# Each load of q, k and v issued as two transfers of four heads

## The chip, the cores and the metric

The kernel runs on one core of a Trainium2 chip. The metric is the device time of one execution in microseconds (us), the median of several runs. Profiles are of one execution each. Engines are named as in the profile: PE (TensorE, matmuls; PEld its weight loads), DVE (VectorE), ACT (ScalarE), POOL (GpSimd) and SP (SyncE, here only an issuer of DMAs). DMAs issued by POOL and by SP are moved by the same 16 transfer engines.

## The reference

Block attention with a Sinkhorn-sorted choice of blocks, and then a token-mixing MLP on its output. Batch B = 4, heads H = 8, sequence S = 768, head size D = 64, 8 blocks of 96 positions.

```python
P = sort_net                                   # [B, H, 8, 8]
for _ in range(5):
    P = exp(P - max(P, -1)); P = P / sum(P, -1); P = P / sum(P, -2)
k_sorted = einsum('bhij,bhjcd->bhicd', P, k blocks)
v_sorted = einsum('bhij,bhjcd->bhicd', P, v blocks)
attn = softmax(scale * q_block @ k_sorted_block^T)
x = (attn @ v_sorted_block) as [B, S, H*D]
wq, wk = x @ w_q, x @ w_k
mixed = (scale * wq @ wk^T) @ x
out = relu(mixed) @ w_out                      # [4, 768, 512], float32
```

## The kernel before

All of q, k and v is read from HBM once, a batch element at a time: twelve loads (`Qn`, `Kn`, `Vn` for each of four batch elements), each of eight heads by 768 positions by 64, float32 in HBM and bfloat16 on the chip. A load puts its 128 partitions by 8 heads by 384 elements into one tile. Each of the three tensors has three buffers (`NIN = 3`), so the load of batch element 3 takes the buffers of element 0 again.

The Sinkhorn steps run on a 32 x 64 tile `Pm` on DVE and ACT (`u_a`, `u_c`, lines 164 to 184) and end in the transposes `PbT`. Meanwhile POOL fills constants (`u_i`): the identity `idb`, zero columns, ones, and at the end `Lx` (lines 194 and 195), which spreads P over partitions. PE meanwhile runs 40 filler matmuls on a zero tile `fil` (`u_Z`). Then `spread` (`u_B`) multiplies `PbT` by `Lx` into PSUM; DVE makes from it the mixing tiles `M` of batch element 0 (`u_n`, `spread_m`, line 233), and ACT copies the rest to `PTR`, from which POOL makes the `M` tiles of the later elements, two heads at a time.

After that PE does, for two heads at a time (a unit `n` of 0 to 3 covers heads 2n and 2n+1): `u_Q` transposes Qn, `u_K` and `u_V` multiply Kn and Vn by `M` (sorting the blocks), `u_F` transposes V back, `u_S` makes scores, ACT exponentiates them (`u_e`), `u_P` multiplies by V, DVE normalises (`u_x`). For batch elements 0 and 1 `u_V` works per pair of heads; for 2 and 3 it reads all eight heads of a third of the rows. Then follow the MLP's units (`u_T`, `u_J`, `u_W`, `u_G`, `u_H`, `u_O`) and the output.

The order is written out by hand in `ORDER` (lines 18 to 51). Each item is unit, batch element, part, and engine or PSUM bank: `l0.1@P` is the load of K for batch element 0 on POOL (0 = q, 1 = k, 2 = v). Every engine works through its own items in that order. The loads stand on POOL's queue in the order K0, V0, Q0, Q1, K1, V1, K2, Q2, then the two weights `wqk` (`m0.0`, `m0.1`), V2, Q3, K3, V3 and the weight `wo` (`m0.2`). Between them stand POOL's constants and its `M` tiles: M of `n1.3` before K1; `n2.0` after it; `n1.0` after V1; `n1.2` after K2; `n1.1`, `n2.1` and `n2.2` after Q2; `n2.3` after wqk; `n3.0` after K3; `n3.3`, `n3.1` and `n3.2` after wo.

The framework adds the waits: a reader of a tile waits for its writer, a writer for the readers before it. For the completions of POOL's DMAs it has eight semaphores, which the DMAs take in turn; an issue whose semaphore has been used before waits on POOL until the DMA that used it has landed.

The end of the kernel (from line 465) checks the row sums and, only if one is out of range, computes all again in another way; in the profiled executions that branch is not taken.

Of the kernel before, what the change touches and what calls it, by code (L numbers as in the profile page):

```python
# [56 lines left out]
def kernel(  # L57
# [11 lines left out]
    nc = tc.nc  # L69
    B, H, S, D = q.shape  # L70
# [3 lines left out]
    P = 128  # L74
# [32 lines left out]
    NIN = 3  # L107
# [129 lines left out]

    def u_l(b, n, e):
        t, src = (Qn, Kn, Vn)[n], (q, k, v)[n]
        nc.gpsimd.dma_start(out=t[b % NIN].rearrange("p h r d -> p h (r d)"),  # L240
                            in_=src[b].rearrange("h (p r) d -> p h (r d)", p=P))

    def u_m(b, n, e):
        if n < 2:
# [206 lines left out]
    for item in ORDER.split():  # L451
        kind, b, n, arg = UNIT.match(item).groups()
        b, half = int(b), halves.get(n[-1], ())
# [22 lines left out]
    with tc.If(redo > 0, preferred_fallthrough_block=False):  # L476
# [12 lines left out]
        for b in range(B):  # L489
            for n in range(3):  # L490
                nc.gpsimd.dma_start(out=(Qn, Kn, Vn)[n][0].rearrange("p h r d -> p h (r d)"),
                                    in_=(q, k, v)[n][b].rearrange("h (p r) d -> p h (r d)", p=P))
            if b == 0:
                spread(1, 0, H)
                src = PS[:, 1, 0:NB * H].rearrange("p (i h) -> p h i", h=H)
            else:
                src = PTR.rearrange("p i h -> p h i")[:, (b - 1) * H:b * H, :]
# [84 lines left out]
```

## Time and profile before

| what | value |
|---|---|
| time, median of 3 runs | 108.27 us (107.89 to 108.35) |
| time of the profiled execution | 108.6 us |
| its span, first to last instruction | 106.8 us |
| mean granted TensorE clock | 0.981 |
| DMA packets and bytes | 18501, 18.57 MB, mean 174 GB/s |
| queue of POOL's DMAs (q0) | 14064 packets, 10.09 MB, 62.8% of 16 engines' span |
| instruction queue (q8) | 14 packets, 0.23 MB |
| loads of K, V, Q: issue to landing, median | 12.8, 14.7 and 15.1 us |

A page begins with the busy share of each engine; a second part cuts the span into 40 slices and gives the busy tenths of each engine and of the DMA engines. The chain that ended last is followed back from the last instruction, at each step to what released it; its shares say which engine sets the end. A line of a timeline has the start, the time taken, engine, source line, operation, tiles (out <- in), how many were merged, and in brackets the idle time of the engine before it and what ended that. A line of the waits has who waited, for whom, the sum in us, how often, and the longest. "issue" there means that the profile shows nothing that the engine waited for. Many lines of PE carry line 149, a helper through which all matmuls go; there the tiles tell them apart.

### The profile page before, as it was taken

The page shows a single profiled execution, that of the slowest core. Times are in us where ns is not written, and L with a number is a line of the kernel's source. Part 1 is how long each engine was busy: PE and PEld are TensorE (multiplying, and loading weights), DVE is VectorE, ACT ScalarE, POOL GpSimd, SP SyncE. Part 2 cuts the span into 40 slices and gives each one's busy share as a digit, 9 for nine tenths or more (in the row PEclk, how much of TensorE's full clock was granted, in tenths as well). Part 3 has the DMA queues.
Part 4 walks back from the last instruction along what each step waited for, and adds up shares of the span by engine and source line. Part 5 has one row for each costly group of instructions (what it writes and reads, how often), then busy time and mean ns, then how long its engine had stood idle before and what let it go on. Part 6 is the DMA issues. An engine that isn't in the chain of part 4 may idle for free.

```text
span 106.8 us, 3637 instructions
## 1 busy us (share of the span) xinstructions
PE 94.2 (88%) x1556; PEld 65.7 (61%) x1556; DVE 74.1 (69%) x144; ACT 69.9 (65%) x101; POOL 31.3 (29%) x51
## 2 busy tenths in 40 slices
PE   5999989597698979889999999999999999999600
PEld 2334489486686966779868867597666565454300
DVE  2687689198797785788989977999767765455200
ACT  4101079769687879898879798688933448784400
POOL 5999089999229400000000000000077000000000
PEclk9999999999999999999999999999999999999975
DMA  0899999999999999999975373100059145496950
GB/s 3 91 201 205 203 203 210 200 203 205 205 204 204 188 202 211 198 203 208 205 161 159 94 211 96 44 6 0 6 196 388 45 196 203 160 408 236 381 196 18
DMA packets 18501, 18.57 MB, mean 174 GB/s; under 512 B 1840, under 2 KB 16560, under 8 KB 18480
## 3 DMA queue, kind: packets, MB, share of 16 engines
q0 software_dynamic: 14064, 10.09, 62.8%
q1 hardware_dynamic: 4416, 8.19, 22.0%
q8 instruction: 14, 0.23, 0.9%
q14 instruction: 7, 0.06, 0.1%
HBM read 20.19 MB, written 6.29 MB: 248 GB/s over the span
## 4 chain that ended last, share of the span: by engine, by line
PE 80%; ACT 6%; issue 4%; DVE 3%; DVEq 0%; ACTq 0%
PE ps L149 80%; ACT E L339 3%; DVE X L364 1%; ACT Vs L153 1%; DVE KT L155 1%; ACT XT L153 1%; ACT QT L153 1%; ACT ot L153 1%; DVE M L233 0%; DVE wk L155 0%; DVE fil L170 0%; DVE RS L362 0%; DVE Pm L169 0%; DVEq L155 0%; ACTq L153 0%
## 5 line engine op out<-in xcount | busy, mean ns | idle before, releaser
L339 ACT ACTIVATE E<-ps 96x960 bf16<-96x960 f32 (+1 forms) x28 | 24.6, 905 | 2.9 <-PE ps L149 2.6
L149 PE MATMUL ps<-wo,mixT 128*128 128x512 bf16 (+1 forms) x100 | 22.9, 371 | 0.0
L364 DVE TENSOR_TENSOR X<-ps,RS 96x896 bf16<-96x896 f32 (+1 forms) x20 | 20.1, 1007 | 0.7
L149 PEld LDWEIGHTS <-mixT 128*128 128x128 bf16 x100 | 8.9, 98 | 8.6 <-issue 0.2
L153 ACT COPY ot<-ps 128x512 f32<-128x512 f32 (+1 forms) x16 | 8.8, 560 | 8.1 <-PE ps L149 4.7
L468 POOL TENSOR_SCALAR ok<-RS 96x280 bf16<-96x280 f32 x1 | 0.9, 924 | 41.9 <-DVE RS L362 41.9
L149 PE MATMUL ps<-fil 128*128 128x512 bf16 x40 | 11.7, 466 | 1.2 <-DVE fil L170 1.2
L149 PE MATMUL ps<-VT,E 96*128 96x65 bf16 x256 | 11.2, 194 | 1.4 <-DVE X L364 0.8
L149 PEld LDWEIGHTS <-E 96*128 96x128 bf16 x256 | 9.8, 97 | 3.6 <-issue 1.5
L149 PE MATMUL ps<-QT,KT 64*128 64x96 bf16 x256 | 9.9, 204 | 1.6 <-issue 1.3
L233 POOL TENSOR_TENSOR M<-PTR,m_p 128x256 bf16<-128x256 bf16 x12 | 8.8, 750 | 7.4 <-PE ps L149 4.1
L155 DVE COPY ot<-ps 128x512 f32<-128x512 f32 x9 | 6.1, 691 | 6.1 <-PE ps L149 3.2
L149 PEld LDWEIGHTS <-fil 128*128 128x128 bf16 x40 | 4.5, 116 | 7.9 <-issue 3.8
L153 ACT CAST KT<-ps 128x768 bf16<-128x768 f32 x10 | 7.7, 805 | 2.0 <-PE ps L149 1.9
L149 PEld LDWEIGHTS <-KT 64*128 64x128 bf16 x256 | 6.8, 94 | 2.9 <-issue 1.6
L149 PE MATMUL ps<-idb,X 96*128 96x96 bf16 x128 | 7.5, 206 | 0.6 <-issue 0.6
L149 PE MATMUL ps<-M,Kn 128*64 128x128 bf16 x192 | 7.5, 221 | 0.3 <-issue 0.3
L155 DVE COPY QT<-ps 128x768 bf16<-128x768 bf16 x13 | 6.7, 551 | 1.4 <-PE ps L149 1.1
L425 ACT ACTIVATE mixT<-ps 128x1024 bf16<-128x1024 f32 x7 | 7.0, 1026 | 0.9 <-PE ps L149 0.6
L149 PEld LDWEIGHTS <-X 96*128 96x128 bf16 x128 | 6.2, 98 | 1.9 <-issue 0.9
L155 DVE COPY VT<-ps 96x1024 bf16<-96x1024 bf16 x7 | 4.8, 687 | 3.5 <-PE ps L149 2.7
L149 PE MATMUL ps<-idb,Qn 128*64 128x128 bf16 x192 | 7.0, 220 | 0.1
(78 smaller groups left out, 154.0 us busy)
## 6 DMA issues: line engine op xcount, KB each, us to landing
out_dram<-ot SPq DMA_DIRECT2D x9, 512.0 KB, 2.8
Kn<-in_k_dram POOLq DMA_DIRECT2D x4, 768.0 KB, 12.8
Vn<-in_v_dram POOLq DMA_DIRECT2D x4, 768.0 KB, 14.7
Qn<-in_q_dram POOLq DMA_DIRECT2D x4, 768.0 KB, 15.1
VT<-Vs SPq DMA_DIRECT2D x12, 130.0 KB, 2.5
out_dram<-ot SPq DMA_DIRECT2D x6, 256.0 KB, 2.7
wo<-in_moe_w_out_dram POOLq DMA_DIRECT2D x1, 512.0 KB, 22.7
qD<-qkT SPq DMA_DIRECT2D x6, 48.0 KB, 2.6
```

Source lines behind the costliest of these rows:

```text
L149: nc.tensor.matmul(o, w, x, is_transpose=t, start=start, stop=stop, skip_group_check=True)
L153: nc.scalar.copy(o, i)
L155: nc.vector.tensor_copy(o, i)
L233: ENG[e].tensor_tensor(out=M[b % 2][:, h0:h1], in0=src[:, h0:h1].unsqueeze(2).to_broadcast([P, 2, SP, NB]), in1=m_p.unsqueeze(1).unsqueeze ...
L339: nc.scalar.activation(E[b % 2][:, n, 0:2 * w * BLK].rearrange("p (t a c) -> p a t c", a=2, c=BLK), PS[0:BLK, bank:bank + 2, 0:w * BLK].re ...
L364: nc.vector.tensor_mul(xo.rearrange("p (a t d) -> p a t d", a=2, d=D), ps[:, :, :, 0:D], rs.unsqueeze(3).to_broadcast([BLK, 2, w, D]))
L425: nc.scalar.activation(o, i, ACT.Relu)
L468: nc.gpsimd.tensor_scalar(out=okf, in0=rsf, scalar1=1e-30, scalar2=None, op0=ALU.is_ge)
```

## The change

`u_l` issues each load as two transfers, heads 0 to 3 and heads 4 to 7, one right behind the other on POOL, in place of one. `ORDER`, tiles, buffers and all else stay.

```diff
     def u_l(b, n, e):
         t, src = (Qn, Kn, Vn)[n], (q, k, v)[n]
-        nc.gpsimd.dma_start(out=t[b % NIN].rearrange("p h r d -> p h (r d)"),
-                            in_=src[b].rearrange("h (p r) d -> p h (r d)", p=P))
+        for h in range(0, H, H // 2):
+            nc.gpsimd.dma_start(out=t[b % NIN][:, h:h + H // 2].rearrange("p h r d -> p h (r d)"),
+                                in_=src[b][h:h + H // 2].rearrange("h (p r) d -> p h (r d)", p=P))
```

The twelve loads become 24 transfers. The branch that computes all again has its own loads, which stay whole.

## The prediction

> **What bounds the kernel now.** I read the page first: the busy shares, the DMA row of the 40 slices, and the chain that ended last.
>
> ```profile
> PE 94.2 (88%) x1556; PEld 65.7 (61%) x1556; DVE 74.1 (69%) x144; ACT 69.9 (65%) x101; POOL 31.3 (29%) x51
> ...
> DMA  0899999999999999999975373100059145496950
> ...
> PE 80%; ACT 6%; issue 4%; DVE 3%; DVEq 0%; ACTq 0%
> ```
>
> TensorE (PE) is 80% of the chain that sets the end. The transfer engines are as good as full from slice 3 to slice 20, some 5 to 53 us, but no DMA stands in the chain: the loads are dense, and yet nobody on the chain waits for one. Whether that is so has to be checked load by load, so I read PE's timeline where each load is used first.
>
> ```profile
> 12.86 0.37 PE L149 MATMUL ps<-PbT,Lx 32*128 32x16 bf16 x8
> 13.62 1.20 PE L149 MATMUL ps<-M,Vn 128*64 128x128 bf16 x36 [0.40 <-DVE M L233]
> 14.63 0.53 PE L149 MATMUL ps<-M,Kn 128*64 128x128 bf16 x12
> ...
> 16.77 0.86 PE L149 MATMUL ps<-idb,Qn 128*64 128x128 bf16 x24
> ...
> 18.57 0.68 PE L149 MATMUL ps<-QT,KT 64*128 64x96 bf16 x23
> 20.54 0.20 PE L149 MATMUL ps<-QT,KT 64*128 64x96 bf16 x1 [1.29 <-issue]
> ...
> 22.02 1.20 PE L149 MATMUL ps<-idb,Qn 128*64 128x128 bf16 x36
> ...
> 26.78 1.20 PE L149 MATMUL ps<-M,Kn 128*64 128x128 bf16 x36
> ```
>
> Issue time plus time to landing, load by load from the DMA view, gives K0 8.7, V0 12.6, Q0 16.4, Q1 21.1, K1 24.9, V1 28.7, K2 32.7, Q2 36.6, V2 41.4, Q3 45.3, K3 49.1 and V3 53.0 us. First uses on PE: V0 13.62 (it waited for M of VectorE, not for V), K0 14.63, Q0 16.77, Q1 22.02, K1 26.78, V1 30.73, K2 39.28, Q2 40.23, V2 45.27, Q3 50.99 and V3 56.11. Every load is there before its use, Q0 by only 0.3 us. PE's waits that follow no engine are these:
>
> ```profile
> PE ps L149 <- issue: 3.2, 5, 1.3
> PE ps L149 <- DVE fil L170: 1.2, 1, 1.2
> PE ps L149 <- DVE X L364: 0.8, 1, 0.8
> ```
>
> The five "issue" gaps (1.29, 0.58, 0.40, 0.56 and 0.32 us) lie 128 weight loads apart, at 20.5, 26.5, 32.5, 39.0 and 45.0 us. Each follows the move of a 16 KB packet on the instruction queue (one starts at 18.22, 24.24, 30.21, 36.62 and 42.65), so PE there waits for its own next block of instructions, whose fetch shares the engines with the loads. None comes after the loads end. Last, GpSimd (POOL), which issues all loads:
>
> ```profile
> 1.29 1.13 POOL L240 DMA_DIRECT2D Kn<-in_k_dram  x1 [0.84 <-POOLq L566]
> ...
> 3.03 0.92 POOL L240 DMA_DIRECT2D Vn<-in_v_dram  x1
> 3.94 0.88 POOL L240 DMA_DIRECT2D Qn<-in_q_dram  x1
> ...
> 8.18 0.88 POOL L240 DMA_DIRECT2D Qn<-in_q_dram  x1
> 9.04 0.54 POOL L194 MEMSET Lx<- 32x512 bf16 x1
> 9.66 0.83 POOL L195 TENSOR_SCALAR_AFFINE_SELECT Lx<-Lx 32x512 bf16<-32x512 bf16 x1
> 13.66 0.75 POOL L233 TENSOR_TENSOR M<-PTR,m_p 128x256 bf16<-128x256 bf16 x1 [3.17 <-ACT PTR L153]
> ...
> 22.34 0.81 POOL L246 DMA_DIRECT2D wqk<-in_moe_w_q_dram  x1
> 23.15 0.75 POOL L246 DMA_DIRECT2D wqk<-in_moe_w_k_dram  x1
> ```
>
> POOL works without a pause from 1.29 to 10.49, where Lx is done. Lx is what PE needs at 12.86. That is the one place where more issuing work on POOL lies near the path.
>
> **What the change gains.** The first four heads of each load land about half a load earlier. Loads land 3.86 us apart, so that is 1.9 us. By the list above nobody waits for any load, so this gain is worth 0. What hides it is PE's own work; if that cover were gone, Q0 would be the first to matter, by its 0.3 us. The bytes, the number of data packets and their order stay as they are. POOL issues its first transfer some 0.15 us sooner (half of the first load), and that too goes to landings that nobody waits for.
>
> **What it adds on POOL.** Twelve more issues. No row shows a half load of four heads, so its price is bounded by the nearest rows. Whole loads (eight rows of 128) cost 0.88 to 0.95 us, the first one 1.13; the three transfers with four rows of 128, wqk twice and wo, cost 0.81, 0.75 and 0.77, mean 0.78. Lower end: 0.46, a whole load divided, with no net cost. Upper end: 0.94, a half as dear as a whole. The shape is that of the wqk and wo rows, so I stay with them; whole loads before 10 us cost about 4% less than later ones, so a half there is 0.75, and the first one 0.98.
>
> Up to Lx that is K0 1.73 for 1.13, V0 1.50 for 0.92, Q0 and Q1 1.50 for 0.88 each: +0.60 +0.58 +0.62 +0.62 = +2.42 us. Lx is then done at 10.49 + 2.42 = 12.91, and PE sees it 0.05 later (M of VectorE ends at 13.57, PE starts at 13.62): 12.96 in place of 12.85, where PE came free of its fillers. **Cost on the path: +0.11 us.** Eight halves at 0.81 make it 0.48 more, +0.59; at 0.73 or less it is nothing. Behind the first Lx matmul stand the M tiles and then all of PE's stream, so a delay here goes to the end one to one.
>
> Lx moves along VectorE's chain, too. The tensor_tensor of L180 at 9.81 took 0.72 us, 0.21 elsewhere; it ended 0.04 after POOL's affine_select of Lx. With Lx's select from about 12.1 on, it meets no two-operand operation of the Sinkhorn chain (the last would end near 11.8), and PbT is ready at 12.1 instead of 12.63. That is worth 0, since the fillers hold PE to 12.85. If the select came early enough to catch L182, PbT would still be there by about 12.8.
>
> The Trainium skill ("SBUF — State Buffer", Who interferes with whom) has a rule for this row: a VectorE instruction with two SBUF inputs and a GpSimd instruction that reads SBUF exclude each other for a whole instruction; by it 0.51 us comes off that chain, and the sum stays the same.
>
> **The new waits.** The program's order shows eight semaphores, taken in turn, for POOL's transfers. Before, the ninth transfer is wqk; now it is the first half of K1, and each issue waits for the landing of the eighth transfer before it. Walking POOL's queue with 0.78 per half and the landings above: K1, V1, K2 and Q2 find theirs landed (Q2's second half asks for Q1, 21.1, at about 22.4). Then the second half of V2 waits until 28.7, Q3 until 30.7 and 32.7, K3 until 34.6 and 36.6, V3 and wo no longer. Queued behind them are M tiles: n1.1 ends near 24.0 (19.4 before) and K1 of those heads is used near 27.5; n2.3 near 27.6, used from 45.3; the last of batch 3 near 42.7 (36.0 before), used from 55.2 (K3). The nearest slack is 3.5 us, so 0. Seven halves, some 13 us of moving, are always queued, so the engines do not run dry. SP's queue gets nothing new, and PE gets some eleven more semaphore conditions on instructions that it already has: between 0 and 11 x 17 ns, what a semaphore instruction takes on POOL, and taken as 0.
>
> **What it adds in the transfer queue.** Twelve more completions. The completion packets take 22 ns in the trace, and packets of neighbouring loads follow without a gap; that is 0.02 us a transfer. The upper bound is the nearest pair of small transfers: wqk's two land at 37.0 and 37.4, 0.4 us apart with their data. At 0.02 nothing is late; at 0.4, see the rivals.
>
> The Trainium skill ("DMA: Bandwidth & Descriptors", Anatomy of one DMA) charges about 2.0 us a transfer plus bytes over 436 GB/s, and its rules say to make transfers larger. Taken as time in the queue, 2.0 for each of the twelve extra transfers would be an estimated 24 us of load stream; the two wqk landings, 0.4 us apart, say that it overlaps with what is queued.
>
> **Sum.** 0 + 0.11 + 0 + 0.02: +0.13 us. The profiled execution took 108.6 us with a span of 106.8; it becomes 108.7. Against the median of 108.27 (0.3 below the profiled one) that is **108.4 us**. Its own range is 108.1 to 108.9.
>
> **The rivals.**
> *POOL decides the start (slower).* If a half costs what a whole does, 0.88 to 0.94, eight issues against four cost 0.88 + 0.92 + 0.88 + 0.88 = 3.56 more; Lx is done at 14.05, PE starts at 14.10 rather than 12.85: +1.25, 109.5 us. It begins to cost at 0.74 us a half and passes 0.5% at 0.80. For it: the price is mostly fixed by the wqk and wo rows, and POOL has no pause there. Against it: those rows are 0.15 below the loads'.
> *Each transfer has a price in the queue (slower).* At 0.4 us, and a start 0.15 sooner, Q0's second half lands 3 x 0.4 later, at 17.5 against a use near 17.1; Q1's, four later, at 22.5 against 22.0; V1's, six later, at 31.0 against 30.7. The worst single lateness counts, not the sum: 0.5, with what Lx adds about +0.7, 109.0. Against it: the 22 ns packets and the full DMA row.
> *Shorter instruction fetches (faster).* The fetch starts about 3.7 us after PE enters a block while loads run, and 0.4 to 1.3 us afterwards; if it waits for a transfer's share on its engine to finish, halves take up to 1.9 us off, and all five gaps close: -3.2, 105.2 us; at 0.5 us off, 0.5 + 0.5 + 0.4 + 0.5 + 0.3 = -2.2, 106.2. Against it: for the five fetches whose engine can be told, the packet goes out 41, 16, 48, 48 and 16 packets after a load's start on that engine, not at an end (64), so whole transfers are not what it waits for; a fixed depth of packets already taken in fits as well, and halves do not change it.
> *The halves bring nothing because both land together.* Same time as the forecast.
>
> **Numbers.** Forecast 0.47, POOL at the start 0.19, price in the queue 0.09, fetches 0.20 (half of it with all gaps closed), the rest, spread evenly, 0.05. A change under 0.5% (0.54 us) is about what cannot be told from none. Faster: the fetches and part of the rest, 0.22. Slower: both slow rivals, a twentieth from the forecast's upper end and part of the rest, 0.34. Same: 0.44. The range is 106.3 to 109.6: it takes in the dear half and the partly closed gaps, and leaves out the fully closed ones (0.10) and what lies beyond 109.6 (0.06).
>
> **What would show it.** Half issues on POOL at 0.73 to 0.81; Lx's select ending near 12.9; PE's first Lx matmul between 12.86 and 13.1; L180 at 0.21 each time; five "issue" gaps of PE of 3 us together; loads still 3.9 us apart; M of n1.1 done by 25. I am wrong if Lx is done after 13.4, if the "issue" gaps shrink or grow by over 0.5 us together, or if a matmul waits for Qn, Kn or Vn.

## The result and the profile after

The changed kernel took 109.12 us (median of 6 runs, 108.82 to 109.47) against 108.21 us for the kernel before (6 runs, 107.89 to 108.35): a ratio of 1.0087, 95% interval 1.0059 to 1.0116. It is slower, by some 0.9 us. The forecast was 108.4 us, a change too small to be told from none; the time lies inside the range, but beyond the forecast's own 108.1 to 108.9, on the slow side.

The profiled execution of the changed kernel took 109.47 us with a span of 107.6 us. Its page, the lines that answer to those shown of before:

```profile
PE 93.9 (87%) x1549; PEld 66.7 (62%) x1556; DVE 73.6 (68%) x144; ACT 69.9 (65%) x101; POOL 38.4 (36%) x63
...
DMA  0899999999999999999956274100049145396950
...
PE 71%; POOL 10%; ACT 5%; issue 5%; DVE 3%; POOLq 0%; ACTq 0%
```

The engines do the same work (PE 93.9 us for 94.2), only POOL has 7.1 us and 12 instructions more. POOL now holds 10% of the chain, which looks as if POOL's issues set the start, as one of the rivals had it. The timelines show what became of that. First POOL, up to Lx, and the second half of V2 (start, time taken, what; in brackets the idle time before and what ended it):

```profile
1.29 1.75 POOL L241 DMA_DIRECT2D Kn<-in_k_dram  x2 [0.83 <-POOLq L567]
...
3.57 1.53 POOL L241 DMA_DIRECT2D Vn<-in_v_dram  x2
5.07 1.51 POOL L241 DMA_DIRECT2D Qn<-in_q_dram  x2
...
9.93 1.48 POOL L241 DMA_DIRECT2D Qn<-in_q_dram  x2
11.39 0.55 POOL L194 MEMSET Lx<- 32x512 bf16 x1
12.02 0.83 POOL L195 TENSOR_SCALAR_AFFINE_SELECT Lx<-Lx 32x512 bf16<-32x512 bf16 x1
...
28.83 0.74 POOL L241 DMA_DIRECT2D Vn<-in_v_dram  x1 [1.02 <-DMA Vn<-in_v_dram]
```

A pair of halves takes 1.48 to 1.53 us once POOL is warm, and Lx is done at 12.85. PE's timeline, at the first Lx matmul, at 20.7 us and then between 44 and 46 us:

```profile
12.91 0.37 PE L149 MATMUL ps<-PbT,Lx 32*128 32x16 bf16 x8 [1.23 <-POOL Lx L195]
13.68 1.20 PE L149 MATMUL ps<-M,Vn 128*64 128x128 bf16 x36 [0.40 <-DVE M L233]
...
20.68 1.09 PE L149 MATMUL ps<-idb,XT 128*96 128x128 bf16 x16
...
44.33 0.33 PE L149 MATMUL ps<-M,Kn 128*64 128x128 bf16 x6
45.67 0.36 PE L149 MATMUL ps<-M,Kn 128*64 128x128 bf16 x6 [1.01 <-issue]
```

The same stretch of the kernel before:

```profile
44.33 0.33 PE L149 MATMUL ps<-M,Kn 128*64 128x128 bf16 x6
44.98 0.36 PE L149 MATMUL ps<-M,Kn 128*64 128x128 bf16 x6 [0.32 <-issue]
```

At the start PE is 0.06 us later than before (13.68 for 13.62). At 20.7 us that is gone: the first weight load of the block of instructions that PE used to wait for there starts at 20.67 and 20.68 us. At 44.33 us they are still level to the hundredth. One matmul later the changed kernel is 0.69 us behind, and it keeps that to the end (PE's last weight load 99.86 before, 100.54 after). So nearly all of the visible loss (0.69 of 0.76 us of span) is one pause of PE that grew from 0.32 to 1.01 us, and it is of the kind called "issue": PE waiting for its next block of instructions. The sum of such pauses conceals it:

```profile
PE ps L149 <- issue: 2.7, 5, 1.0
```

It was 3.2 us in five before. One pause fell out (the one at 20.5 us), another tripled, and the sum went down while the kernel became slower. (The fifth of after is 0.16 us at 89.95 us, among the `wo` matmuls, of which the trace has only 93 of 100 records.)

### The profile page after: what moved, and what is told of

Its sections match the earlier page's. It is cut to its first block, busy times and chain, and to the rows that moved or that the text cites. A ratio compares the mean times of both kernels' runs of the same rounds, so it can differ in the third digit from the quotient of the medians.

```text
span 107.6 us, 3643 instructions
## 1 busy us (share of the span) xinstructions
PE 93.9 (87%) x1549; PEld 66.7 (62%) x1556; DVE 73.6 (68%) x144; ACT 69.9 (65%) x101; POOL 38.4 (36%) x63
## 4 chain that ended last, share of the span: by engine, by line
PE 71%; POOL 10%; ACT 5%; issue 5%; DVE 3%; POOLq 0%; ACTq 0%
PE ps L149 71%; ACT E L340 3%; POOL Qn L241 3%; POOL Vn L241 1%; ACT Vs L153 1%; POOL Kn L241 1%; POOL E L204 1%; DVE X L365 1%; DVE KT L155 1%; POOL Lx L195 1%; ACT QT L153 1%; POOL VT L206 1%; ACT ot L153 1%; POOL Lx L194 0%; POOL E L203 0%
## 5 line engine op out<-in xcount | busy, mean ns | idle before, releaser
L149 PE MATMUL ps<-wo,mixT 128*128 128x512 bf16 (+1 forms) x93 | 22.2, 370 | 0.5 <-issue 0.2
L149 PE MATMUL ps<-fil 128*128 128x512 bf16 x40 | 10.4, 427 | 1.2 <-DVE fil L170 1.2
L149 PE MATMUL ps<-M,Kn 128*64 128x128 bf16 x192 | 8.6, 241 | 1.0 <-issue 1.0
L149 PEld LDWEIGHTS <-Kn 128*64 128x64 bf16 x192 | 6.9, 123 | 1.7 <-issue 1.2
L241 POOL DMA_DIRECT2D Kn<-in_k_dram x8 | 6.3, 793 | 3.2 <-PE ps L149 1.2
## 6 DMA issues: line engine op xcount, KB each, us to landing
Vn<-in_v_dram POOLq DMA_DIRECT2D x8, 384.0 KB, 11.7
```

Of the source, the lines that this page charges most:

```text
L149: nc.tensor.matmul(o, w, x, is_transpose=t, start=start, stop=stop, skip_group_check=True)
L241: nc.gpsimd.dma_start(out=t[b % NIN][:, h:h + H // 2].rearrange("p h r d -> p h (r d)"), in_=src[b][h:h + H // 2].rearrange("h (p r) d -> ...
```

## The experiments

In each study the kernel before ran on the same chip beside the new ones (median 108.27 to 108.29 us); ratios are to it.

**First theories.** B: Lx is late, so POOL sets the start. A: POOL's own instruction fetch, which its 12 additional instructions moved to 43.3 us in the trace, collides there with PE's. C: the additional waits and completions of all the halves cost a little each. Three kernels: only the first four loads split; only the last eight; and no load split, but POOL given one tiny instruction behind each load.

```diff
+        step = H // 2 if (b, n) in ((0, 0), (0, 1), (0, 2), (1, 0)) else H   # e1; "not in": e2
+        for h in range(0, H, step):
...
         nc.gpsimd.dma_start(...)                                              # e3: load whole
+        nc.gpsimd.memset(gate, 0.0)
```

> Only K0, V0, Q0 and Q1 are split, the four loads that POOL issues ahead of Lx; the other eight stay whole. Theory A (POOL's twelve more instructions pull a fetch of POOL's next instruction block from about 84 us into the load stream, at 43.3 us, and PE's own block fetch goes out 0.67 us later beside it): four more instructions, no POOL fetch between 36 and 46 us, +0.0 to +0.2 us against the kernel before. Theory B (Lx is late at the start, 12.86 for 10.49 us): Lx ends near 12.9 us again, the full +0.8 us. Theory C (the waits for the eight semaphores and the extra completions slow the loads): about a third, +0.2 to +0.3 us.

> K0, V0, Q0 and Q1 stay whole, the eight loads after Lx are split. Lx ends at 10.5 us. A: eight more POOL instructions; if they are enough for POOL's extra fetch to fall between 38 and 46 us, +0.6 to +0.8 us, else 0. B: 0.0 us. C: +0.5 to +0.8 us, with POOL's waits for landings at V2, Q3 and K3 as in the changed kernel.

> All loads whole as before, and behind each load POOL writes one element of a scratch tile: twelve more POOL instructions, no more transfers. A: POOL's extra fetch comes inside the load stream, a few us earlier than in the changed kernel since POOL has no waits for landings here; +0.3 to +0.8 us if it meets a fetch of PE's (36.6 or 42.7 us), near 0 if it falls between them. B: four writes of about 0.1 us ahead of Lx, which ends near 10.9 us: 0.0 us. C: 0.0 us.

Measured: e1 108.37 us, ratio 1.0012 (1.0000 to 1.0024); e2 109.13, 1.0074 (1.0051 to 1.0096); e3 108.36, 1.0004 (0.9987 to 1.0021). In e1 Lx is as late as in the full change:

```profile
12.01 0.83 POOL L195 TENSOR_SCALAR_AFFINE_SELECT Lx<-Lx 32x512 bf16<-32x512 bf16 x1
```

and next to nothing is lost; in e2, where Lx is done at 10.43 as before, nearly all is. B falls. e3 does not decide A: its POOL fetch went out at 36.9, not at 43 us.

**Lx early.** The full change, with Lx built right behind Q0's issues, ahead of POOL's other constants.

```diff
-l0.1@P i0.0@P c0.0@D l0.2@P a0.1@A c0.1@D l0.0@P i0.2@P ...
-a0.4@A i0.3@P c0.4@D ...
+l0.1@P i0.0@P c0.0@D l0.2@P a0.1@A c0.1@D l0.0@P i0.3@P i0.2@P ...
+a0.4@A c0.4@D ...
```

> The whole change, but POOL makes Lx right after Q0's issues, ahead of the other constants and of Q1's load. Lx ends near 8.0 us, PE starts with PbT at 12.2 to 12.9 us. A: POOL's fetch at 43 us as in the changed kernel, still +0.6 to +0.9 us. B: 0.0 us or a gain of up to 0.2. C: +0.6 to +0.9 us.

Measured: 109.23 us, 1.0075 (1.0051 to 1.0099), with Lx done 4.85 us sooner:

```profile
7.17 0.83 POOL L195 TENSOR_SCALAR_AFFINE_SELECT Lx<-Lx 32x512 bf16<-32x512 bf16 x1
```

B falls for the second time.

**POOL's fetch beside PE's.** e5 is the full change with 20 tiny instructions on POOL behind Lx, so that POOL's fetch comes early. e6 is the kernel before with POOL held, ahead of V3's issue, until a value of X is there; e7 is e6 with nine tiny instructions more, which bring POOL's fetch to 43 us without a split load.

```diff
+            for j in range(20):                                   # e5, behind Lx
+                nc.gpsimd.memset(pad[:, j:j + 1], 0.0)
...
-... n3.0@P x1.4@D t0.2@A K2.0@4 l3.2@P ...
+... n3.0@P x1.4@D N1.4@x t0.2@A K2.0@4 l3.2@P ...                 # e6, e7
...
+        for j in range(9):                                        # e7, in N1.4
+            nc.gpsimd.memset(pad[:, j:j + 1], 0.0)
```

> The whole change, and 20 one-element writes of POOL into a scratch tile behind Lx, so that POOL reaches the end of its instruction block some 15 us earlier. A (POOL's block fetch beside PE's): POOL's fetch moves from 43.3 us to some 25 to 30 us, PE's fetch after 39 us goes out 3.7 us after PE enters its block again, not 4.4, and the time falls to +0.0 to +0.3 us against the kernel before, unless the two fetches meet at the new place. C (waits for semaphores, extra completions, queue of halves): nothing of that changes, +0.7 to +0.9 us.

> Whole loads as before; POOL reads one element of an X tile of batch element 1 ahead of V3's issue, so that V3, wo and the last three M tiles run near 39.3 to 43 us, as in the changed kernel, with two more POOL instructions. A: no POOL fetch in the load stream, 0.0 to +0.1 us. C, in the form that late issues on POOL slow PE's fetch: +0.6 us or more.

> As the kernel with the read of X, and nine more one-element writes of POOL ahead of it, so that POOL crosses its block at V3's issue near 39 to 40 us. A: POOL's fetch near 43 us, PE's fetch late by some 0.7 us beside it, +0.5 to +0.8 us against the kernel before, with whole loads and no extra transfer. C: the same time as the kernel without the nine writes, within 0.2 us.

Measured: e5 109.00 us, 1.0065 (1.0042 to 1.0087), with POOL's fetch at 22.0 us; e6 108.57, 1.0009 (0.9983 to 1.0036); e7 108.27, 1.0000 (0.9983 to 1.0018), with POOL's fetch at 43.4 us. The pause of PE, e5 first, then e7:

```profile
45.39 0.36 PE L150 MATMUL ps<-M,Kn 128*64 128x128 bf16 x6 [1.01 <-issue]
```

```profile
44.45 0.36 PE L150 MATMUL ps<-M,Kn 128*64 128x128 bf16 x6 [0.33 <-issue]
```

The long pause is there without POOL's fetch, and POOL's fetch is there without the long pause. A falls from both sides.

**Fewer instructions on POOL.** The full change, with the constants of KT, VT and Vs written by VectorE and the last three `M` tiles of batch element 3 made in one instruction: a second way to move POOL's fetch (it came at 79.0 us), which also starts the stream sooner.

```diff
+            for t in KT:                                          # c0.0, on VectorE
+                nc.vector.memset(t[:, :, S:S + P - BLK], 0.0)
...
-                nc.gpsimd.memset(t[:, :, S:S + P - BLK], 0.0)      # i0.2; VT and Vs likewise
...
-        h0, h1 = 2 * n, 2 * n + 2
+        h0, h1 = (2, H) if (b, n) == (3, 3) else (2 * n, 2 * n + 2)
```

> The whole change with eight POOL instructions fewer: the constants of KT, VT and Vs are written by DVE while it waits for its first input, and the last three M tiles of batch element 3 are one instruction. A: POOL's fetch leaves the load stream (near 78 us), 0.0 to +0.2 us against the kernel before. C: +0.7 to +0.9 us. B, if the start mattered after all: Lx ends about 1 us sooner, at most -0.1 us.

Measured: 108.45 us, 1.0014 (0.9990 to 1.0037). It seems to be a cure, but the pause is as long as ever:

```profile
44.92 0.36 PE L149 MATMUL ps<-M,Kn 128*64 128x128 bf16 x6 [1.02 <-issue]
```

Lx is done at 11.57, PE's V0 matmuls begin at 12.75 in place of 13.62, and the gain is given back at 44.9 us. Two effects of opposite sign; the time alone would have told a false story.

**What the slow kernels share.** Left over was C, but e1, with a third of the additional waits, lost 0.1 us. So I looked at PE's records that are no matmuls: its separate semaphore instructions, 51 ns each. In the traces before and after they stand, within PE's stream of the first 60 us, at

```
before   26.48          40.34
after    26.49   39.62  40.35
```

The one at 39.62 belongs to K2. Its heads 4 and 5 are the second unit of K2 that PE takes. Their first weight load already waited for VectorE, which makes X out of what their PSUM bank held before; with K2 split, it has to wait for the landing of the second half, too. No weight load or matmul in these traces carries more than one condition. The load kept the landing, which was at 32.6 us, and the wait for VectorE became an instruction of its own. VectorE's instruction in after:

```profile
38.90 0.69 DVE L365 TENSOR_TENSOR X<-ps,RS 96x512 bf16<-96x512 f32 x1
```

It ends at 39.58, so that condition was met just ahead of the semaphore instruction. PE is hardly stopped: the matmul ahead of it starts at 39.59 and the next weight load at 39.70. But the fetch of PE's next instruction block starts 3.70 us after it, not 3.69 us after PE's entry into the block. That is theory K: the semaphore instruction, 0.66 us behind the block's start, holds the request for the next block back by as much.

**Theory K against C.** e9: all split but K2. e10: K2 alone. e11: all split, K2 into six heads and two, so that the two conditions meet on heads 6 and 7, at the end of the block. e12: e8 with K2 whole.

```diff
+        step = H if (b, n) == (2, 1) else H // 2                   # e9, e12; e10: the reverse
+        for h in range(0, H, step):
...
+        m = 6 if (b, n) == (2, 1) else H // 2                      # e11
+        for h0, h1 in ((0, m), (m, H)):
```

> The change with one load left whole: K2 (K of batch element 2); the other eleven loads stay split. Open so far: in every kernel that lost 0.7 us, PE's fetch of the instruction block that it needs at 45 us starts 4.3 to 4.4 us after PE entered the block before, in all others 3.7. In the slow ones PE has one more semaphore instruction, at 39.6 us, because the first weight load that reads K2's second half has to wait for VectorE (its PSUM bank) and for the landing of that half, two conditions on one instruction. Theory K: that separate instruction, 0.66 us behind the block's start, holds PE's sequencer, and the request for the next block goes out that much later. Then here: no semaphore instruction near 39.6, fetch 3.65 to 3.75 after the block's start, issue gap near 45 us of 0.3 to 0.6, ratio to before 0.999 to 1.003. Theory C (what is lost comes from many more completions and waits in all, or from half loads in the queue): eleven twelfths of the loss stay, ratio 1.006 to 1.008, fetch 4.3 or later.

> The kernel before with one load split: K2 alone. Theory K: the extra semaphore instruction of PE stands near 39.6 us, the fetch starts 4.3 to 4.4 us after the block's start, the issue gap near 45 us is 0.65 us longer, ratio 1.005 to 1.008: one split load costs what twelve do. Theory C: one twelfth of the loss, ratio 0.999 to 1.002, fetch 3.7.

> The change with all twelve loads split, but K2 into six heads and two. The first weight load of K2's heads 4 and 5 then has VectorE alone to wait for; the double condition moves to heads 6 and 7, some 104 weight loads further on, at the end of the same instruction block. Theory K (the place of the semaphore instruction close behind the block's start is what costs): no semaphore instruction near 39.6, one near 44.5, fetch 3.65 to 3.75 after the block's start, ratio 0.999 to 1.003. Rival K2 (one instruction more in that block costs, wherever it stands): fetch 4.3 or later, ratio 1.005 to 1.009. Theory C: the same as K2, 1.006 to 1.008.

> A version that may beat both: the kernel with fewer instructions on POOL (the constants of KT, VT and Vs written by VectorE, three M tiles of the last batch element in one instruction), whose stream started 0.6 to 0.9 us sooner and which then lost it again at the late fetch (ratio 1.0014), with K2 left whole. Theory K: fetch 3.65 to 3.75 after the block's start, the sooner start is kept, ratio 0.992 to 0.998. Theory C: ratio 1.000 to 1.002 as before.

Measured: e9 108.45 us, 1.0021 (1.0006 to 1.0036); e10 109.18, 1.0079 (1.0059 to 1.0099); e11 108.38, 1.0006 (0.9991 to 1.0022); e12 107.19, 0.9915 (0.9884 to 0.9947). PE's pause in e9, e10 and e11, in this order:

```profile
44.72 0.36 PE L149 MATMUL ps<-M,Kn 128*64 128x128 bf16 x6 [0.32 <-issue]
```

```profile
45.69 0.36 PE L149 MATMUL ps<-M,Kn 128*64 128x128 bf16 x6 [1.00 <-issue]
```

```profile
44.91 0.36 PE L149 MATMUL ps<-M,Kn 128*64 128x128 bf16 x6 [0.51 <-issue]
```

Eleven split loads cost some 0.2 us (by the interval 0.1 to 0.4), the twelfth by itself costs what all twelve do, and with the same twelve loads split the cost goes once the semaphore instruction stands at 43.94 us, when the fetch is already under way (from 42.51). C falls, and so does the rival that an instruction more in that block costs wherever it is. The pause in e11 is 0.2 us longer than in e9 (its fetch came 3.82 us behind the entry rather than 3.77, and PE resumed 2.40 us after the fetch's start rather than 2.26); that doesn't show in the times. Both fetches, and the ratio of e12, lie a little outside the figures that were expected under K (3.65 to 3.75 us; 0.992 to 0.998).

All kernels in one table, from their traces: PE's entry into the block (its 608th weight load), the semaphore instruction of K2 where there is one, the start of the 16 KB packet on the instruction queue, and PE's entry into the next block, in us.

| kernel | entry | semaphore | fetch starts | next block | ratio |
|---|---|---|---|---|---|
| before | 38.96 | | 42.65 | 44.98 | |
| e1 | 38.69 | | 42.35 | 44.71 | 1.0012 |
| e3 | 38.71 | | 42.46 | 44.73 | 1.0004 |
| e6 | 38.96 | | 42.62 | 44.99 | 1.0009 |
| e7 | 38.43 | | 42.12 | 44.45 | 1.0000 |
| e9 | 38.69 | | 42.46 | 44.72 | 1.0021 |
| e11 | 38.69 | 43.94 | 42.51 | 44.91 | 1.0006 |
| e12 | 37.92 | | 41.62 | 43.95 | 0.9915 |
| after | 38.96 | 39.62 | 43.32 | 45.67 | 1.0087 |
| e2 | 38.70 | 39.37 | 43.10 | 45.42 | 1.0074 |
| e4 | 38.95 | 39.61 | 43.32 | 45.67 | 1.0075 |
| e5 | 38.68 | 39.34 | 43.02 | 45.39 | 1.0065 |
| e8 | 38.20 | 38.87 | 42.58 | 44.92 | 1.0014 |
| e10 | 38.98 | 39.64 | 43.34 | 45.69 | 1.0079 |

In the rows without an early semaphore instruction the fetch starts 3.66 to 3.82 us after the entry. In the last six it starts 4.34 to 4.40 us after the entry, and 3.68 to 3.73 us after the semaphore instruction.

**The version that beats both** is e12, at 107.19 us, 0.85% below the kernel before. It starts sooner and keeps it:

```profile
12.22 0.37 PE L149 MATMUL ps<-PbT,Lx 32*128 32x16 bf16 x8
12.99 1.20 PE L149 MATMUL ps<-M,Vn 128*64 128x128 bf16 x36 [0.40 <-DVE M L234]
...
43.29 0.34 PE L149 MATMUL ps<-M,Kn 128*64 128x128 bf16 x6
43.94 0.36 PE L149 MATMUL ps<-M,Kn 128*64 128x128 bf16 x6 [0.32 <-issue]
```

It differs from e8 in K2 alone, and e8 was 1.26 us slower (108.45); of that the traces show 0.97 at the next block (44.92 to 43.95): the late request's 0.7, and an entry 0.28 sooner. PE's entries into this block differ by steps of about 0.27 us between kernels that do the same up to there (38.43, 38.70, 38.97). Whether the same change of constants without any split load does as well wasn't tried.

## Why the prediction was wrong where it was

- **The step that failed** is the one on new waits: "PE gets some eleven more semaphore conditions on instructions that it already has: between 0 and 11 x 17 ns [...] and taken as 0". PE has twelve more waits on POOL's DMAs. Eleven went onto instructions that were free to carry them (nine weight loads, two matmuls), and e9 prices all eleven splits at some 0.2 us. The twelfth met a wait for VectorE on the same weight load, and one of the two became an instruction. Its own 51 ns would have been harmless, even within my bound. What went with it was a fetch of the next instruction block that started 0.67 us later, at a time when PE had no slack to that block; e10 priced it at 0.85 us (0.64 to 1.07), the trace of after at 0.69 (6.71 us from block to block, 6.02 before). The traces don't place the 0.2 us that are left of the 0.9.
- **The view that held the answer** was the program's order of PE, with its waits: the list of before against the list of after, looking for instructions with two conditions. I counted the conditions and did not look where two meet.
- **The rival on instruction fetches** was near it. It took PE's pauses while loads run for waits on the fetch and gave the 3.7 us from entry to fetch; but I looked only for what halves might take off that, and put a price on no way to lengthen it. The halves did not shorten the fetch: with K2 whole it still starts 3.77 us after the entry.
- **Right: the price of a half.** Forecast 0.75 us, 0.98 for the first; measured 0.75 to 0.78 up to Lx (0.74 to 0.80 over all), and 1.75 for the first two together. Lx was forecast at 12.91 and done at 12.85; the first Lx matmul, forecast at 12.96, started at 12.91. L180 took 0.21 us each time, as forecast.
- **Right in size, but not charged rightly: the late Lx.** I charged its delay "to the end one to one". PE's stream was 0.06 us late at 13.68 and level at 20.7. So small a shift is lost among the fetches: e9, with its first Lx matmul at 12.91, enters the block at 38.69, and e10, with 12.61, at 38.98. e4 shows that Lx earlier by 4.85 us brings nothing either, since the fillers then hold PE to 12.83. A start that moves by 0.6 us, as in e12, does carry through. That the fillers end at 12.92 us, on which the +0.11 rests, holds for one execution only: in the fourteen traces they end between 11.40 and 13.00, in after at 11.68. In e2, e7 and e10, with Lx and the fillers done early, PE started on `PbT` at 12.61 to 12.63, 0.3 us ahead of after. So it is in part luck that the two profiles differ by only 0.05 us there.
- **Right: POOL's waits for its semaphores.** The second half of V2 waited (1.02 us, to 28.83), M of n1.1 was done at 23.45 (forecast 24.0), the last M of batch 3 at 42.71 (42.7). No matmul waited for Qn, Kn or Vn.
- **Right: no price in the queue.** Halves landed 1.94 us apart, half of the loads' 3.86 (K0 complete at 8.4, Q0 at 16.2, Q1 at 20.8, V1 at 28.5 us). Neither rival that costs the queue or the start had a part in the result.
- **The sum without the failed step** would have held: e9 and e11, which have eleven and twelve split loads and no early semaphore instruction, are 0.16 and 0.09 us slower than before by their medians; forecast +0.13. e11's interval includes no change, e9's just doesn't.
- **My own test was too coarse.** I said that I would be wrong if the pauses together changed by over 0.5 us. They changed by 0.5, downwards, while one grew by 0.69.
- **Luck.** The upper end of the range, 109.6 us, was set for half issues as dear as whole ones. These did not come; the loss that lies inside the range has another cause.

What stays open is why a semaphore instruction has this effect. It may be its place, 0.66 us behind the entry; it may as well be that it waits. In all six slow kernels it starts 0.04 us after VectorE's X is done, so the wait for VectorE, held in an instruction of its own, may be what kept the request back. The other such instructions don't part the two: the one at 40.34, 1.4 us behind the entry, which every kernel has, waits for a load of `wqk` that had landed by 37.4 us; the one of e11, 5.25 us behind the entry, does wait, for ScalarE, but the fetch has started by then. That PE's sequencer runs ahead of PE, and sends the request on its way, would fit; no run measured that. Nor is 3.7 us the rule for every block: in the one ahead (entered at 32.49 before) the fetch starts 3.85 to 4.13 us after the entry in all fourteen kernels, with no semaphore instruction of its own in it.

## What to carry to other kernels

When a transfer is split, list the first readers of the new part on each engine, and look for one that now has two things to wait for: one of the two becomes an instruction, even if the new part has long landed. Where PE shows pauses that follow nothing, at even distances and with a packet on the instruction queue ahead of them, PE is paced by its instruction fetch: a start that moves by some hundredths can't be followed through it, and a separate semaphore instruction close behind a block's start can cost its distance from that start (here 0.7 us, with a wait for VectorE that had only just ended). Read such pauses one by one, since their sum can fall while the kernel gets slower.

## What the runs showed of the hardware

**The clock after a pause of PE at the start.** In three kernels (the changed one, e11, e9) PE's fillers ended at 11.5 to 11.7 us and PE then waited 1.23, 1.27 and 1.38 us for Lx. The granted clock was 0.52 in the stretch from 14.7 to 18.2 us, where the kernel before had 1.00. The windows view, 14.7 to 18.2 us, of after and then of before (busy time and count of PE, PEld, DVE, ACT, POOL; PEclk; DMA share; GB/s):

```profile
14.70:18.20 3.50, 3.50 (x61) 3.19 (x57) 1.73 (x3) 2.54 (x4) 3.48 (x6) 0.52 1.31 202
```

```profile
14.70:18.20 3.50, 3.50 (x112) 3.30 (x108) 3.04 (x5) 3.29 (x6) 3.46 (x5) 1.00 1.32 204
```

PE got through 61 matmuls instead of 112, and had caught up by 20.7 us, since the kernel before stood waiting for instructions for 1.29 us in between. e2, e5, e10 and e7 waited 1.04, 1.18, 1.21 and 1.22 us at the same place, up to 12.6 to 12.9, and kept a clock of 1.00. The three that lost it are the three that waited longest, so the length of the pause may decide it; the values lie too close for these traces to show it. The fillers end at different times for a like reason: they start 0.43 us apart at first and 0.22 us apart later, and the clock rises to 1.00 at 4.0 to 7.3 us, at another moment in each execution.

**Instruction fetch.** PE's pauses lie 128 weight loads and 128 matmuls apart, each behind a 16 KB packet on the instruction queue. While the 16 transfer engines are full they come to 3.2 us before the change, with a fetch that starts some 3.7 us after the block's start. The Trainium skill ("Runtime: NRT & Kernel Launch", Instruction fetch mechanics) describes blocks of 16 KiB or 256 instructions that an engine fetches through its own DMA queue while it runs the current one, and says the cost is mostly hidden. The block size agrees with the traces; that the cost is hidden does not.

**A VectorE operation with two inputs from SBUF beside POOL's select** took 0.83 us in e4 (L176, ended 0.05 us after the select of Lx at 8.00), 0.72 in the kernel before (L180) and 0.21 in after, where none met it. The long one moves with Lx.
